# Reordering the head of a cosine-attention + MLP kernel: first pair's copies, third roots and a value load moved earlier

## The chip, the cores and the metric

One core of one Trainium2 chip. The metric is device time in microseconds (us); lower is better. Every run also lists the mean clock that TensorE was granted, as a share of full speed. All times below are in us unless marked otherwise.

## The reference, cut to what matters

```python
# q, k, v: (8 batches, 12 heads, 448 positions, 64) float32
q_n = q / (norm(q, axis=-1) + 1e-6);  k_n = k / (norm(k, axis=-1) + 1e-6)
attn = softmax(q_n @ k_n^T / 0.1)
x = (attn @ v) -> (3584 tokens, 768)
out = gelu_exact(x @ w_in) @ w_out          # 768 -> 2048 -> 768
```

## The kernel before

The kernel handles two heads at a time, a "pair"; six pairs make a batch. For each pair it squares queries and keys, sums the squares per row, takes roots, scales and rounds to bf16 (a 16-bit float), transposes (TensorE, then a copy by VectorE out of PSUM, the memory that TensorE writes to), multiplies scores, takes exponentials (ScalarE), and multiplies by the values. Then the batch goes through the MLP, whose first product is called `hp`. From the second batch on, all this preparation lies under dense matmuls of the MLP. Only in the first batch, about the first 38 us, is TensorE short of work. It is filled there with dummy matmuls, `spin`.

The code counts from 0, the texts count ordinals from the first: "third roots" and "third scaling" belong to index 2 (`roots(3)` brings the number done to three), and "squares of pair 3" are those of index 3, the only whole pair's squares on VectorE (of pair 0 it has the queries). "Sums" (`reduce`) are the sums of squares per row, on VectorE. A root is taken on ScalarE as half a logarithm and then an exponential, and VectorE makes its reciprocal, so "fourth logarithm" is the start of the fourth root. `upto(f, n)` calls `f` until `n` calls are done. In these traces each engine's instructions stand in the order in which they are written here.

```python
def square(g):
    ...
    elif g <= 2:
        nc.scalar.activation(sq, t, AF.Square)
    elif g == 3:
        nc.vector.tensor_tensor(sq, t, t, ALU.mult)     # two SBUF inputs
    else:
        nc.gpsimd.tensor_tensor(sq, t, t, ALU.mult)

def scale(g):          # two halves, queries and keys; all on GpSimd but half of pair 0
    ...
    for i, eng in enumerate((nc.vector if g == 0 else nc.gpsimd, nc.gpsimd)):
        eng.tensor_tensor(qkb[:, i]..., t[:, i], rn[:, i].to_broadcast(...), ALU.mult)

def spin(n):
    ...
    ps = mm_tile("spin")
    for _ in range(n):
        nc.tensor.matmul(ps[:CS, :S], lhsT=ident, rhs=blank, start=True, stop=True)

def attention_first():
    ...
    for g in range(HP):                       # HP = 6 pairs
        scores(g, 0)
        if g == 0:
            upto(square, 4)
            upto(reduce, 4)
            roots(3)
            upto(scale, 3)
            scores(g, 2, 1)
        if g < HP - 1:
            upto(transposes, g + 2)
        ...                                   # spin, value sums, scores(g, 2 or 3)
        upto(load_v, (2, 3, 3, 3, 3, 4)[g], NV)
        upto(load_wi, (1, 2, 3, 4, 4, 4)[g])
        ...
    ...                                       # the last values of the batch

# main program
...
upto(load_qk, 5)
spin(24)
...
upto(load_v, 1, NV)
upto(square, 1); upto(reduce, 1); roots(1); upto(square, 3); upto(scale, 1); upto(reduce, 2)
roots(2)
upto(scale, 2)
upto(load_v, 2, NV)
upto(load_wi, 1)
upto(transposes, 1)
spin(5)
upto(reduce, 3)
...                                           # attention_first, MLP, next batches
```

Values (`load_v`) and weights (`load_wi`) are loaded by GpSimd, each issue costing it about 0.8 us. `load_v` number 0 covers pair 0, number 1 pairs 1 and 2, number 2 pairs 3 to 5.

## Time and profile before

| | before |
|---|---|
| time, median of 3 (range) | 440.19 (439.91 to 441.44) |
| profiled run, granted clock | 439.89, 0.999 |
| first queries landed = VectorE's first squares start | 4.58 |
| first exponential starts | 12.75 |
| first MLP product `hp` starts | 38.52 |

The landing of the first queries varies between runs by up to 0.65 us whatever the kernel. So times of the head are compared below as distance from that landing: `hp` starts 33.95 after it here.

First, three stretches of 2 us of this kernel, from the view by stretches. The columns are the stretch and its length, busy time and instruction count of PE, PEld, DVE, ACT and POOL, then PEclk, the DMA share and GB/s:

```profile
14.00:16.00 2.00, 1.84 (x16) 0.97 (x14) 1.93 (x5) 1.97 (x5) 0.68 (x2) 1.00 1.12 235
16.00:18.00 2.00, 1.00 (x8) 0.51 (x9) 0.73 (x3) 1.97 (x5) 2.00 (x3) 1.00 1.13 236
18.00:20.00 2.00, 2.00 (x14) 1.09 (x15) 0.80 (x2) 1.08 (x2) 2.00 (x2) 1.00 1.25 236
```

Second, three rows of TensorE's timeline (start, length, engine, line, operation, tiles, shapes, count): two groups of fillers and the first `hp`.

```profile
14.87 0.96 PE L323 MATMUL spin<-blank,ident 112*112 112x448 bf16 x4
18.21 0.92 PE L323 MATMUL spin<-blank,ident 112*112 112x448 bf16 x4
38.52 0.74 PE L433 MATMUL hp<-x,wi 128*128 128x448 bf16 x3
```

The clock is full in all three stretches (1.00), and four fillers take 0.92 to 0.96.

### The profile page before, as it was taken

What the parts mean: (1) busy time and instruction counts of PE and PEld (TensorE: products, weight loads), DVE (VectorE), ACT (ScalarE), POOL (GpSimd) and SP (SyncE); (2) the same over time, 40 slices, a digit from 0 to 9 for tenths busy, and PEclk for the clock granted to TensorE, in tenths of its full rate; (3) what the DMA queues carried; (4) which work ended last, traced back from release to release, by engine and by line L of the source; (5) the groups of instructions that cost most, each with busy time, mean ns of one, the idle gap of its engine ahead of it and who ended that gap; (6) DMA issues with size and microseconds to landing.
All of it is one profiled execution on the core that took longest, in us unless ns stands there. A gap on an engine that the chain in (4) does not pass through costs nothing.

```text
span 438.1 us, 7927 instructions
## 1 busy us (share of the span) xinstructions
PE 426.8 (97%) x3294; PEld 215.7 (49%) x3294; DVE 164.8 (38%) x266; ACT 264.0 (60%) x380; POOL 203.3 (46%) x185
## 2 busy tenths in 40 slices
PE   7789999999999999999999999999999999999996
PEld 4344554445445554455544545445444554445563
DVE  4776313641355305552154501753055421341021
ACT  4796587646666467744767359655766457773300
POOL 2899834491834609291571906655190722300000
PEclk9999999999999999999999999999999999999999
DMA  9999999946683909766295843748077600911022
GB/s 201 237 241 209 180 178 211 265 105 135 109 160 88 226 4 114 171 119 149 29 159 134 159 109 53 172 121 208 1 130 153 134 2 1 132 43 31 1 72 72
DMA packets 83635, 54.97 MB, mean 125 GB/s; under 512 B 41872, under 2 KB 78608, under 8 KB 83600
## 3 DMA queue, kind: packets, MB, share of 16 engines
q1 hardware_dynamic: 66416, 42.35, 43.4%
q0 software_dynamic: 16784, 11.80, 19.1%
q8 instruction: 25, 0.41, 0.4%
q10 hardware_dynamic: 400, 0.33, 0.2%
q14 instruction: 10, 0.08, 0.1%
HBM read 45.61 MB, written 11.01 MB: 129 GB/s over the span
## 4 chain that ended last, share of the span: by engine, by line
PE 90%; DMA 5%; POOL 2%; DVE 1%; ACT 1%; SPq 0%; issue 0%; DVEq 0%
PE op L268 35%; PE hp L433 33%; PE st L206 11%; PE o L228 7%; PE sm L228 4%; DMA qk<-in_k_dram 3%; DMA v<-in_v_dram 2%; POOL qkb L176 1%; POOL sq L137 1%; SPq L107 0%; ACT pt L209 0%; DVE nq L149 0%; DVE x L246 0%; DVE rs L239 0%; DVE ot L279 0%
## 5 line engine op out<-in xcount | busy, mean ns | idle before, releaser
L209 ACT ACTIVATE pt<-st 112x896 bf16<-112x896 f32 x192 | 165.1, 913 | 50.0 <-PE st L206 49.6
L268 PE MATMUL op<-wo,g 128*128 128x384 bf16 x896 | 157.9, 327 | 0.0
L433 PE MATMUL hp<-x,wi 128*128 128x448 bf16 x768 | 147.0, 353 | 0.2 <-DVE x L246 0.2
L455 ACT ACTIVATE g<-hp 128x448 bf16<-128x448 f32 x128 | 66.9, 545 | 89.9 <-PE hp L433 89.6
L268 PEld LDWEIGHTS <-g 128*128 128x128 bf16 x896 | 81.9, 98 | 70.0 <-issue 21.0
L433 PEld LDWEIGHTS <-wi 128*128 128x128 bf16 x768 | 74.5, 98 | 72.1 <-issue 3.7
L176 POOL TENSOR_TENSOR qkb<-qk,rn 112x512 bf16<-112x512 f32 x95 | 96.8, 1045 | 11.8 <-DVE rn L167 11.7
L137 POOL TENSOR_TENSOR sq<-qk 112x1024 f32<-112x1024 f32 x44 | 82.3, 1888 | 5.8 <-DMA qk<-in_k_dram 5.6
L165 POOL TENSOR_SCALAR se<-sr 112x48 f32<-112x48 f32 x14 | 4.6, 326 | 150.2 <-ACT sr L164 150.2
L149 DVE TENSOR_REDUCE nq<-sq 112x16 f32<-112x1024 f32 x47 | 57.0, 1214 | 38.7 <-POOL sq L137 38.6
L206 PE MATMUL st<-qkT 64*112 64x448 bf16 x384 | 59.7, 374 | 2.6 <-ACT pt L209 1.9
L279 DVE COPY ot<-op 128x384 f32<-128x384 f32 x55 | 29.8, 543 | 79.2 <-PE op L268 79.2
L167 DVE RECIPROCAL rn<-se 112x48 f32<-112x48 f32 (+1 forms) x20 | 7.9, 393 | 99.7 <-POOL se L165 99.4
L228 PE MATMUL o<-pt,v 112*32 112x448 bf16 x768 | 41.8, 353 | 1.0 <-DMA v<-in_v_dram 1.0
L206 PEld LDWEIGHTS <-qkT 64*112 64x112 bf16 x384 | 21.5, 124 | 38.3 <-issue 34.5
L246 DVE TENSOR_TENSOR x<-o,rs 128x448 bf16<-128x448 f32 x48 | 27.8, 620 | 5.0 <-PE o L228 2.7
L228 PEld LDWEIGHTS <-v 112*32 112x32 bf16 x768 | 20.3, 97 | 17.1 <-DMA v<-in_v_dram 1.2
L235 DVE STREAM_TRANSPOSE tr<-sm 128x448 f32<-128x448 f32 x24 | 15.5, 646 | 34.8 <-PE sm L228 34.8
L228 PE MATMUL sm<-pt,ones 112*32 112x448 bf16 x384 | 23.1, 355 | 0.0
L323 PE MATMUL spin<-blank,ident 112*112 112x448 bf16 x46 | 13.3, 439 | 2.9 <-DVE qkT L194 1.5
L239 DVE STREAM_TRANSPOSE rs<-rc 128x448 f32<-128x448 f32 x24 | 15.5, 645 | 0.8
L120 POOL DMA_DIRECT2D v<-in_v_dram x17 | 14.0, 823 | 0.0
(37 smaller groups left out, 80.0 us busy)
## 6 DMA issues: line engine op xcount, KB each, us to landing
qk<-in_q_dram SPq DMA_DIRECT2D x48, 224.0 KB, 5.8
qk<-in_k_dram SPq DMA_DIRECT2D x47, 224.0 KB, 6.1
v<-in_v_dram POOLq DMA_DIRECT2D x15, 336.0 KB, 6.8
wi<-in_moe_w_in_dram POOLq DMA_DIRECT2D x4, 768.0 KB, 11.5
wo<-in_moe_w_out_dram POOLq DMA_DIRECT2D x4, 768.0 KB, 20.7
out_dram<-ot SPq DMA_DIRECT2D x7, 336.0 KB, 3.5
out_dram<-ot SPq DMA_DIRECT2D x8, 288.0 KB, 2.6
out_dram<-ot SPq DMA_DIRECT2D x8, 240.0 KB, 3.0
```

Of the source, the lines that this page charges most:

```text
L137: nc.gpsimd.tensor_tensor(sq, t, t, ALU.mult)
L149: nc.vector.tensor_reduce(nq, sq, mybir.AxisListType.X, ALU.add)
L176: eng.tensor_tensor(qkb[:, i].rearrange("p c h d -> p h c d"), t[:, i], rn[:, i].to_broadcast([CS, 2, NC, D]), ALU.mult)
L206: nc.tensor.matmul(st[:CS, h, :S], lhsT=qkT[rows, 1, c, :], rhs=qkT[rows, 0, :, :], start=True, stop=True)
L209: nc.scalar.activation(pt, st[:CS, :, :S], AF.Exp, scale=inv_tau)
L228: nc.tensor.matmul(bank_t[g, n][r:r + 32, :S], lhsT=w, rhs=pt_t[g + j, c][:, h, :], start=(c == 0), stop=(c == NC - 1), tile_position=(0, r))
L235: nc.vector.transpose(tr.rearrange("p b r -> p (b r)"), bank_t.pop((g, 0))[:, :S])
L246: nc.vector.tensor_tensor(x_t[b][:, p + n - 1, :], bank_t.pop((g, n))[:, :S], rs, ALU.mult)
L268: nc.tensor.matmul(ps[:, :NH], lhsT=g_t[sb][:, kf, t * 128:(t + 1) * 128], rhs=wo[:, kf, ni * NH:(ni + 1) * NH], start=(kf == 0), stop=(kf ...
L279: nc.vector.tensor_copy(ot[:, lo:hi], ps[:, :NH])
L433: nc.tensor.matmul(hps[m], lhsT=wi[:, kd, m * 128:(m + 1) * 128], rhs=x_t[b][:, kd, :], start=(kd == order[0]), stop=(kd == order[-1]))
L455: nc.scalar.activation(g_t[sb][:, m, hf * S:(hf + 1) * S], hps.pop(m), AF.Gelu)
```

## The change

Its intent: VectorE copies the first pair's transposes while it would else wait for the second pair's root, so scores and exponentials start earlier; the third roots come ahead of the fourth sums, so GpSimd starts the third scaling earlier; value and weight loads move to where GpSimd idles, and the late value load that TensorE waited for is issued about 11.5 us earlier (25.60 before, 14.04 after).

```diff
 attention_first, g == 0:
             upto(square, 4)
-            upto(reduce, 4)
             roots(3)
             upto(scale, 3)
+            upto(load_wi, 1)
             scores(g, 2, 1)
 ...
-        upto(load_v, (2, 3, 3, 3, 3, 4)[g], NV)
+        upto(load_v, (3, 3, 3, 3, 3, 4)[g], NV)
 main program:
     upto(reduce, 2)
+    upto(load_v, 2, NV)
+    upto(transposes, 1)
+    spin(2)
     roots(2)
     upto(scale, 2)
-    upto(load_v, 2, NV)
-    upto(load_wi, 1)
-    upto(transposes, 1)
-    spin(5)
+    upto(load_v, 3, NV)
     upto(reduce, 3)
```

The fourth sums are then written after the first transposes of the second pair (`upto(reduce, ...)` in the loop).

## The prediction

> **What bounds the kernel now.** I read the page's busy shares first, then TensorE's waits after the first batch, then the chain of waits of the first 60 us, then the timeline row by row.
>
> ```profile
> PE 426.8 (97%) x3294; PEld 215.7 (49%) x3294; DVE 164.8 (38%) x266; ACT 264.0 (60%) x380; POOL 203.3 (46%) x185
> PEclk9999999999999999999999999999999999999999
> ...
> core 0: us, PE busy (x) PEld busy (x) DVE busy (x) ACT busy (x) POOL busy (x), PEclk, DMA share, GB/s
> 38.50:438.00 399.50, 395.31 (x3012) 199.63 (x3008) 139.89 (x220) 237.35 (x340) 174.04 (x153) 1.00 0.59 116
> ...
> engine line waited for: us in total, times, longest us
> PE hp L433 <- DVE x L246: 0.2, 1, 0.2
> ```
>
> TensorE is busy 97% at the full granted clock. From 38.5 us, where the first MLP product `hp` starts, to the end, all its waits come to 0.2 us. The change touches only the instructions before that. So its worth is the number of microseconds by which `hp` starts earlier, if nothing later takes them back. At best it is some part of 38.5 us, of which most is work; 2% would be 8.8 us.
>
> The head is a chain that changes engines (start, length, what):
>
> ```profile
> 16.91 0.72 POOL qkb L176
> 17.91 1.88 POOL sq L137
> 19.80 2.00 POOL qkb L176 x2
> 21.80 1.85 POOL sq L137
> 23.65 1.95 POOL qkb L176 x2
> 25.60 7.08 DMA v<-in_v_dram
> 32.73 0.93 PE o L228 x14
> ```
>
> GpSimd works without a gap from 15.9 to 25.6 us, only then issues the value load, and TensorE waits for its landing. Ahead of that, the rows that the reordering concerns:
>
> ```profile
> 10.51 0.18 DVE L160 TENSOR_REDUCE se<-root 112x16 f32<-112x32 f32 x1 [0.97 <-ACT root L159]
> 11.28 1.11 PE L323 MATMUL spin<-blank,ident 112*112 112x448 bf16 x5 [1.54 <-DVE qkT L194]
> 12.56 1.63 DVE L135 TENSOR_TENSOR sq<-qk 112x1024 f32<-112x1024 f32 x1
> 15.91 2.04 POOL L176 TENSOR_TENSOR qkb<-qk,rn 112x512 bf16<-112x512 f32 x2 [1.32 <-DVE rn L167]
> 19.50 1.72 ACT L209 ACTIVATE pt<-st 112x896 bf16<-112x896 f32 x2 [0.92 <-PE st L206]
> 32.73 0.93 PE L228 MATMUL o<-pt,v 112*32 112x448 bf16 x14 [0.96 <-DMA v<-in_v_dram]
> 34.03 3.34 ACT L209 ACTIVATE pt<-st 112x896 bf16<-112x896 f32 x4 [1.08 <-PE st L206]
> ```
>
> VectorE idles 0.97 us for the second pair's root, although the first pair's transposes (done at 9.33 and 9.73) lie ready to be copied.
>
> **What the Trainium skill says.** (1) "Perfetto Trace Analysis", Optimization Strategy: a kernel can have several regimes, and one finds the gaps on the engine that matters in that regime and what releases them. This trace agrees: by the stretches view TensorE is busy 8.36, 6.73 and 16.40 us in 0 to 10, 10 to 20 and 20 to 38.5, so idle for 7.0 us, and almost never after. (13.3 us of that busy time are fillers, the `spin` row of the page.) (2) "SBUF — State Buffer", Who interferes with whom: a VectorE instruction with two SBUF inputs contends with a GpSimd one that reads SBUF; the first to issue holds the shared pair for its whole length. The trace agrees: the squares of pair 3 start on VectorE at 12.56, GpSimd's scaling ends at 13.10, and the squares end at 14.18, 1.08 after that, 1.63 in all. (3) "DMA: Bandwidth & Descriptors", Issuing engines are not separate DMA queues: all loads share 16 engines and interleave. The DMA share is 1.17 at 10 to 20 us and 1.15 at 20 to 38.5, so moving loads redistributes landings and adds no bandwidth. (4) "TensorE: Matmul & The Clock Gate", HAM clock gate: an idle window of about 3.4 us halves the clock. Only three filler matmuls go, and the wait that they border gets shorter; here a wait of 1.54 us left the next ones at 0.19 us spacing, so I give this nothing.
>
> **The change, part by part** (times in us; "b" is before).
>
> 1. First pair's copies first. They fall into the 0.97 wait: first at 9.44 (b 10.89), second at 9.77 to 10.15 (b ends 11.52). The second pair's root still comes at 10.51, so that costs nothing. Fillers go from five to two, 0.19 each: scores start at 10.30 (b 12.31), the first exponential at 10.74 (b 12.75): 2.0 earlier. The second pair's scaling on GpSimd stays at 11.06 to 13.10.
>
> 2. Third roots ahead of fourth sums. The squares of pair 3 now issue at 12.02, but behind the same GpSimd scaling, by point (2): they end at 14.18 as before. Next on VectorE come the third roots (14.10, b 15.35) rather than 1.2 of sums. Their logarithm sits on ScalarE behind two earlier exponentials, done at 12.91, so it is ready. Reciprocal ends 14.57 (b 15.82), third scaling on GpSimd starts 14.65 (b 15.91): 1.25 earlier. The fourth sums end 16.17 (b 15.44), so the fourth logarithm starts at about 16.23 against 16.41: here ScalarE keeps only 0.2 of its 2.0, and idles 1.4 for it.
>
> 3. ScalarE's later wait of 0.92 goes. It stood because the third pair's transposes waited for the scaling; those now end at 16.95, four fillers follow, scores at 17.80, and the exponential follows without a gap at 18.29 (b 19.50).
>
> 4. The weight load leaves the idle time before the third scaling and comes after it, into the solid GpSimd chain: 0.78. Scaling ends 16.69, load to 17.4, squares of pair 4 at 17.43 (b 17.91). So GpSimd's lead shrinks from 1.25 to 0.48. It is also what sets the fifth logarithm (20.63, b 21.11) and all TensorE work to about 31: lead 0.48.
>
> 5. The value load of pairs 3 to 5 goes from 25.60 to about 13.1, in the gap before the third scaling. Two effects. GpSimd is 0.83 shorter between the fifth and sixth scalings, which TensorE doesn't wait for (in before it was still at other matmuls when the sixth scaling ended, 29.25 against 29.42). And the value wait goes. In before the block of 16 matmuls starts at 31.41, stops after two of them until 32.73, and the next scores come at 33.59. With the lead of 0.48 it starts at 30.93 and takes 0.87, as 16 such matmuls do elsewhere in the chain: next scores at 31.80, a lead of 1.79.
>
> 6. Part of this is given back. The next scores wait for exponentials, now in a closed row: 32.36 to 35.69 on ScalarE (b 34.03 to 37.37). The scores that came at 35.81 come at 34.13. But the last value sums need the accumulator that VectorE's normalising frees: third value block 32.80 (b 34.11), normalised by 34.95 (b 36.26), last value block 35.02 (b 36.33). From there 2.19 of dense matmuls: `hp` at 37.21 against 38.52.
>
> Sum: 0.48 from the reordering (1.25 less 0.78 for the weight load), plus 1.31 of value wait, less 0.48 by ScalarE and the accumulator: 1.3.
>
> **Rivals.**
>
> (a) The lock goes the other way: the squares get the pair at 12.10, between two scalings. They end at 13.18, the second scaling's half slips to 14.2, the value load to 15.0, the third scaling starts at 15.05. GpSimd's lead is then 0.08 and the whole gain about 0.9: 439.3. For it: VectorE waits already when the first half ends. Against: the second half is dispatched 0.04 before the first ends.
>
> (b) Later landings don't move along. DMA is saturated to 64 us, its order changes but not its volume. The second output-weight load lands at 56.75 and is needed at 58.6, so at 57.3 after; the transposed tile of pair 9 lands at 70.95 and is first used at 71.53, so at 70.22. If that landing stays, 0.7 is lost and 0.6 is left: 439.6. For it: 6.9 us from issue to landing beside other loads. Against: its issue at 64.08 follows the scaling, which comes earlier too, and the weights ahead are issued earlier as well.
>
> (c) The early value loads push back loads that are needed. The pair-3 keys land at 10.86, before the early load of the second values, issued about 9.3 (a load issued at 6.14 landed only at 14.60), can get in; first input weights have slack: the second of them landed at 36.36, needed now at 37.21, and less lies ahead of it. If wrong, squares on GpSimd wait and the gain is nil: 440.2.
>
> (d) The value wait was the only one that counted, ScalarE closing up everywhere after: 2 or more, 438.2, if the accumulator's 0.4 is hidden too.
>
> **Range and chances.** Centre 1.2: 1.3 with a little off for (a) and (b), so 439.0 from 440.19. The three runs of before spread over 1.5, most within 0.3. Low 438.2 is rival (d), high 440.1 is (c) with its noise. 2% is out of reach either way: the head holds only 7.0 us of idleness and 13.3 of fillers, most of which cover the first loads; and to lose 8.8 the order would have to stall on a load.
>
> **What would show each step.** First exponential at 10.7; squares of pair 3 ending 14.2 (lock as before) or 13.2 (a); third scaling at 14.65; fourth logarithm hardly earlier, with 1.4 of ScalarE idle ahead of it; fifth logarithm 0.5 earlier; no wait on a value load in TensorE's list; a TensorE gap of about 0.4 before the last value block; `hp` at 37.2; after it still about 0.2 of waits. I am wrong if `hp` starts within 0.5 of 38.52, if TensorE's waits after it exceed 0.5, or if its matmuls are slower.

## The result, and the profile after

| | before | after |
|---|---|---|
| median of 4 runs, same rounds (range) | 440.78 (439.91 to 441.44) | 439.72 (439.53 to 440.31) |
| ratio of means, 95% interval | | 0.9979 (0.9955 to 1.0003) |
| granted clock of the runs | 0.999 in the profiled one | 0.991, 0.992, 0.996, 0.990 |
| first landing | 4.58 | 4.93 |
| first exponential, after the landing | 8.18 | 6.22 |
| `hp`, after the landing | 33.95 | 33.97 |

Ratios here and below are the mean time of one kernel's fast runs over that of the other's in the same rounds, so they are not quite the ratios of the medians quoted.

The time lies in the predicted range, but the profile tells another story than the prediction: the first exponential is 1.96 earlier, as predicted, the value wait is gone, and yet `hp`, counted from the landing, starts not a moment earlier. Something in the head ate all of it. The page of the changed kernel, its clock line and PE's busy share:

```profile
PE 428.9 (98%) x3291; PEld 216.1 (49%) x3291; DVE 164.6 (38%) x266; ACT 264.4 (60%) x380; POOL 204.3 (47%) x185
...
PEclk9699999999999999999999999999999999999999
```

PE is busy 2.1 us longer than before (428.9 against 426.8) with three instructions fewer. The second digit of the clock line, about 11 to 22 us, is 6: before it was 9. The view by stretches, the same columns as above:

```profile
14.00:16.00 2.00, 1.85 (x9) 0.99 (x10) 1.26 (x2) 0.82 (x2) 1.99 (x4) 0.52 1.19 243
16.00:18.00 2.00, 2.00 (x10) 0.67 (x9) 0.93 (x3) 1.23 (x4) 1.98 (x3) 0.50 1.24 258
18.00:20.00 2.00, 2.00 (x12) 1.15 (x9) 1.00 (x2) 1.24 (x2) 2.00 (x2) 0.50 1.22 241
20.00:22.00 2.00, 2.00 (x10) 0.83 (x9) 0.84 (x1) 1.21 (x2) 2.00 (x3) 0.77 1.32 248
```

A clock of 0.50 is half speed. The trace's clock record has it from 14.09 to 20.92, that is for 6.83 us (the 0.52 and 0.77 fit: 1.91 and 0.92 us of these two stretches at half speed). TensorE's timeline shows what that does:

```profile
14.15 0.55 PE L192 MATMUL tp<-ident,qkb 112*128 112x112 bf16 x4 [1.33 <-POOL qkb L176]
15.18 1.74 PE L323 MATMUL spin<-blank,ident 112*112 112x448 bf16 x4
18.50 1.70 PE L323 MATMUL spin<-blank,ident 112*112 112x448 bf16 x4
38.90 0.36 PE L433 MATMUL hp<-x,wi 128*128 128x448 bf16 x1
```

Four fillers take 1.74 and 1.70 where they took 0.96 and 0.92. And the chain of waits, which before ran through GpSimd to the value load, now runs through slow fillers:

```profile
4.93 0.70 DVE sq L131
...
11.07 3.03 POOL qkb L176 x2
14.10 0.05 issue
14.15 0.55 PE tp L192 x4
...
15.25 1.67 PE spin L323 x4
...
18.71 1.49 PE spin L323 x4
```

A filler was free while TensorE had nothing to do. At half clock it pushes real work back.

The chain shows a second surprise: the second scaling, two instructions, takes 3.03 in place of 2.04. GpSimd's and VectorE's timelines:

```profile
11.07 3.02 POOL L176 TENSOR_TENSOR qkb<-qk,rn 112x512 bf16<-112x512 f32 x2 [0.68 <-DVE rn L167]
14.87 2.05 POOL L176 TENSOR_TENSOR qkb<-qk,rn 112x512 bf16<-112x512 f32 x2
```

```profile
11.98 1.21 DVE L135 TENSOR_TENSOR sq<-qk 112x1024 f32<-112x1024 f32 x1
```

The squares of pair 3 ended at 13.19 after 1.21; before they took 1.63, because they had to wait for GpSimd. Now it is GpSimd that waits: its second half took 2.02 (12.07 to 14.09) against 1.04 for one elsewhere. That is rival (a).

After the head nothing is given back. TensorE's waits from 37 us to the end are

```profile
PE o L228 <- DVE x L246: 0.2, 1, 0.2
PE hp L433 <- DVE x L246: 0.2, 1, 0.2
```

and every later TensorE instruction stands 0.37 to 0.38 later than in the trace before, about the 0.35 by which the first landing was later. So the whole story lies before `hp`.

### The profile page after: what moved, and what is told of

The parts are those of the page before. It is cut to its first block, busy times and chain, and to the rows that moved or that the text cites. A ratio compares the mean times of both kernels' runs of the same rounds, so it can differ in the third digit from the quotient of the medians.

```text
span 438.5 us, 7921 instructions
## 1 busy us (share of the span) xinstructions
PE 428.9 (98%) x3291; PEld 216.1 (49%) x3291; DVE 164.6 (38%) x266; ACT 264.4 (60%) x380; POOL 204.3 (47%) x185
## 4 chain that ended last, share of the span: by engine, by line
PE 93%; DVE 2%; ACT 2%; POOL 1%; DMA 1%; issue 0%; DVEq 0%; POOLq 0%
PE op L268 35%; PE hp L433 33%; PE st L206 12%; PE o L228 8%; PE sm L228 4%; ACT pt L209 1%; POOL qkb L176 1%; DMA qk<-in_q_dram 1%; PE spin L323 1%; PE tp L192 1%; DVE x L246 0%; DVE nq L147 0%; DVE nq L149 0%; ACT lq L155 0%; POOL v L120 0%
## 5 line engine op out<-in xcount | busy, mean ns | idle before, releaser
L176 POOL TENSOR_TENSOR qkb<-qk,rn 112x512 bf16<-112x512 f32 x95 | 97.8, 1055 | 11.3 <-DVE rn L167 11.0
L206 PE MATMUL st<-qkT 64*112 64x448 bf16 x384 | 60.9, 380 | 1.9 <-ACT pt L209 1.7
```

The costliest lines, as they stand in the source:

```text
L176: eng.tensor_tensor(qkb[:, i].rearrange("p c h d -> p h c d"), t[:, i], rn[:, i].to_broadcast([CS, 2, NC, D]), ALU.mult)
L206: nc.tensor.matmul(st[:CS, h, :S], lhsT=qkT[rows, 1, c, :], rhs=qkT[rows, 0, :, :], start=True, stop=True)
```

## The experiments

The first theory after the result: the change gains about 0.9 to 1.1 in the head, as rival (a) says, and the half clock takes it away again; the clock falls because TensorE is busy too little for too long early in the head. Its rivals: the fall is chance and costs nothing; or the moves themselves are worth nothing, because ScalarE or the landing of loads sets the end. "hp" below is the start of `hp` after the first landing, from the run's profile; a list of clocks is over its runs. By the rule of 2% the verdict of every run in the table is "same"; what follows are smaller differences, read with their intervals and clocks.

| run (chip) | mean of fast runs | ratio (95%) | clocks | hp |
|---|---|---|---|---|
| e1_fill5 (12) | 439.59 | 0.9997 (0.9976 to 1.0018) | 0.994 to 0.998 | 34.36 |
| e2_before_fill2 (12) | 439.80 | 1.0002 (0.9982 to 1.0022) | 0.990 to 0.999 | 33.69 |
| e3_value_only (12) | 439.45 | 0.9996 (0.9967 to 1.0026) | 4 runs 0.999 or 1.0, 2 below | 33.02 |
| e4_order_only (12) | 439.70 | 1.0000 (0.9974 to 1.0026) | 0.996 to 0.999 | 33.51 |
| e0_after_again (11) | 439.83 | 0.9995 (0.9977 to 1.0012) | 0.990 to 0.992 | 34.03 |
| e5_gap_fill (11) | 438.70 | 0.9969 (0.9952 to 0.9986) | 0.999 or 1.0 | 32.88 |
| e6_squares_scalar (11) | 438.43 | 0.9961 (0.9939 to 0.9983) | 0.999 or 1.0 | 32.03 |
| e7_value_earlier (11) | 437.84 | 0.9949 (0.9930 to 0.9969) | 0.998 to 1.0, one slow run | 31.81 (slow run) |
| e8_best_again (3) | 437.61 | 0.9945 (0.9929 to 0.9960) | 0.998 to 1.0 | 31.61 |
| e9_copies_late (3) | 440.02 | 0.9999 (0.9972 to 1.0025) | 3 runs 0.999 or 1.0, 3 below | 34.35 |
| e10_weights_early (3) | 437.40 | 0.9940 (0.9925 to 0.9955) | 0.999 or 1.0 | 31.56 |
| e11_before_filled (3) | 439.19 | 0.9980 (0.9965 to 0.9996) | 0.999 or 1.0 | 33.22 |

The kernel before ran beside them, 11 times on each chip: means 439.71 (chip 12), 440.33 (11), 440.07 (3). Its own clock falls too: 18 of these 33 runs had a clock below 0.998. Their mean is 440.51, that of the other 15 is 439.47. So one fall costs it about 1 us, and "before" is a mix of two states. The mix differs by chip (3, 6 and 9 of 11 runs on chips 12, 11 and 3), so part of a ratio in the table is the clock of the kernel before. The changed kernel fell in all ten runs that it had.

**e1_fill5: the changed kernel with five fillers instead of two.**

```diff
     upto(transposes, 1)
-    spin(2)
+    spin(5)
```

> The changed kernel with five filler matmuls ahead of the first scores again, instead of two. Filler theory: with three fillers fewer TensorE did too little in a window of about 3.4 us before 14.1 us, the clock was halved for 6.8 us and that cost about 1 us; with five the granted clock is back at 0.999 in the runs, first scores about 0.57 later than in the changed kernel, the MLP start at 37.4 to 38.0, time about 0.7 to 1 us below the changed kernel's. Rival, lock theory: the pause comes from the wait of 1.33 us for the second pair's scaling, which GpSimd lost to VectorE's squares; then fillers ahead of it don't matter, the clock still falls to 0.99 and the time is that of the changed kernel or up to 0.5 us more.

The clock still fell, in five of six runs, and not at the same place: in the profile from 23.60 to 27.01. A miss for the idea that the three removed fillers were the cause. Two rows of TensorE's timeline:

```profile
13.97 0.37 PE L192 MATMUL tp<-ident,qkb 112*128 112x112 bf16 x4 [1.23 <-POOL qkb L176]
24.55 0.62 PE L323 MATMUL spin<-blank,ident 112*112 112x448 bf16 x1
```

The gap of 1.23 behind the slow second scaling is still there, and the fillers ahead of the scores delay the exponentials (6.78 after the landing in place of 6.22). The single filler at 24.55 takes 0.62, where one takes 0.35 at full clock.

**e2_before_fill2: the kernel before with two fillers instead of five.**

```diff
     upto(transposes, 1)
-    spin(5)
+    spin(2)
```

> The kernel before with two fillers instead of five at the same place, nothing else. Filler theory: its clock falls too, to 0.990 to 0.996, and it is about 0.5 to 1.5 us slower than before. Rival, lock theory: no squares ahead of the scaling, so the clock stays at 0.999, and the scores come up to 0.57 us earlier, of which at most 0.3 us reaches the end.

The clock fell in five of six runs (in the profile from 13.81 to 17.23), against 3 of 11 of the kernel before on that chip. That points to fillers at this place helping the clock, on few runs. But the mean, 439.80, is no worse than before's 439.71: scores came earlier too (first exponential 7.75 after the landing, before 8.18), and the value wait was 0.6 instead of 1.0. Mixed.

**e3_value_only: the kernel before, only the third value load moved.** It goes with the second, into GpSimd's idle time after the second scaling; the order of everything else stays.

```diff
     upto(scale, 2)
-    upto(load_v, 2, NV)
+    upto(load_v, 3, NV)
     upto(load_wi, 1)
```

> The kernel before with the third value load alone moved into GpSimd's idle time before the third scaling; VectorE's order, fillers and the weight load as before. My sum: the value wait of 1.3 us goes, 0.5 of it given back at the exponentials and the accumulator, so the MLP starts about 0.8 us earlier (37.7), clock 0.999, time 0.8 us below before. Rival, contention theory: the earlier load delays the first weight load or the keys, and less than 0.3 us is left.

GpSimd's timeline has the two loads side by side, and TensorE's has the block of sixteen value matmuls without the stop:

```profile
12.85 1.53 POOL L120 DMA_DIRECT2D v<-in_v_dram  x2
```

```profile
31.21 0.94 PE L228 MATMUL o<-pt,v 112*32 112x448 bf16 x16
```

`hp` starts 0.93 earlier than before. Over all runs the time shows nothing (0.9996), as two of the six had a fallen clock. The four at full clock took 438.48 to 438.94, mean 438.75; the eight full-clock runs of the kernel before on the same chip have a mean of 439.49. So this one line is worth about 0.7 us where the clock holds.

**e4_order_only: the changed kernel with five fillers and the third value load at its old place.**

```diff
-    spin(2)
+    spin(5)
     roots(2)
     upto(scale, 2)
-    upto(load_v, 3, NV)
 ...
-        upto(load_v, (3, 3, 3, 3, 3, 4)[g], NV)
+        upto(load_v, (2, 3, 3, 3, 3, 4)[g], NV)
```

> The changed kernel with five fillers, but the third value load at its old place behind the fifth scaling: the reordering on VectorE and the weight load's place alone. If the squares of pair 3 take the shared pair first, as in the changed kernel's profile (squares end 13.2, second scaling's half takes 2.0 us), GpSimd's lead is about 0.1 us and the time within 0.2 us of before; if my first reading had held (squares end 14.2), 0.5 us below before. The value wait of about 1 us is in TensorE's list again in either.

The value wait is back with 0.8, the second scaling again takes 3.02, the clock fell in four of six runs (half from 14.61 to 18.02 in the profile), and the ratio is 1.0000. Over all runs the reordering without the load shows no gain in time. But `hp` is 0.44 earlier than in the profile before, fallen clock and all, and its two runs at 0.998 and 0.999 took 438.59 and 438.99, mean 438.79, which is 0.7 below the full-clock runs of the kernel before: as much as e3. Two runs do not settle it, so what the reordering is worth alone at full clock stays open.

**e0_after_again and e5_gap_fill: the clock itself.** e0 is the changed kernel, unedited, so that e5 has it on the same chip. e5 adds fillers only where TensorE waits: three ahead of the third scores of pair 0, five ahead of the second pair's transposes (the gap behind the slow scaling), three ahead of the fourth pair's.

```diff
-    def spin(n):
-        ps = mm_tile("spin")
+    def spin(n, aside=None):
+        ps = mm_tile("spin", aside=aside)
 ...
             upto(load_wi, 1)
+            spin(3, 0)
             scores(g, 2, 1)
+        spin((5, 0, 3, 0, 0, 0)[g], 0)
         if g < HP - 1:
             upto(transposes, g + 2)
```

> The changed kernel itself, beside the next three on one chip. Clock below 0.998 in most of its runs, since a window of 3.41 us around 9 to 14 us holds only 0.2 to 0.35 of TensorE streaming whatever the window's phase; time within 0.5 us of before.

> The changed kernel with fillers put where TensorE really waits: three ahead of the third scores of pair 0, five ahead of pair 1's transposes, three ahead of pair 3's. Activity theory (a window with less than about 0.4 of streaming halves the clock for the next): clock at 0.998 or above in most runs, the matmuls after 14 us at their full pace, MLP start 33.0 to 33.2 after the first load's landing as in the kernel with the value load alone, time 0.7 to 1.0 us below the changed kernel's on this chip. Rival (the clock falls with the phase of the run or with the chip, not with activity): clocks and times as for the changed kernel, plus nothing.

e0 repeats the result: clock fallen in six of six runs, half from 13.10 to 19.92 in the profile, `hp` 34.03. e5 held the full clock in six of six. Its fillers at the place of the slow ones, on TensorE's timeline, and its second scaling, on GpSimd's:

```profile
14.61 0.96 PE L323 MATMUL spin<-blank,ident 112*112 112x448 bf16 x4
```

```profile
10.90 3.02 POOL L176 TENSOR_TENSOR qkb<-qk,rn 112x512 bf16<-112x512 f32 x2 [0.99 <-DVE rn L167]
```

The fillers are back at 0.96 while the scaling is as slow as in the changed kernel. So the two effects are told apart. `hp` is 1.15 earlier than in e0, and the mean time 1.13 lower (438.70 against 439.83): the fallen clock cost the changed kernel 1.1 us, all that it had gained. Both runs are on the same chip and the edit adds eleven matmuls, so it is not that less work was done.

**e6_squares_scalar: e5 with the squares of pair 3 on ScalarE**, written behind the third roots, so that no VectorE instruction with two SBUF inputs meets the second scaling.

```diff
-        elif g <= 2:
+        elif g <= 3:
             nc.scalar.activation(sq, t, AF.Square)
-        elif g == 3:
-            nc.vector.tensor_tensor(sq, t, t, ALU.mult)
 ...
-                upto(square, 4)
                 roots(3)
+                upto(square, 4)
```

> The same with the squares of pair 3 on ScalarE, behind the third roots: VectorE then has no instruction with two SBUF inputs beside GpSimd's second scaling. Lock theory: the second half of that scaling takes 1.04 us and not 2.02, the third scaling starts about 1 us earlier than in the changed kernel, the fourth logarithm about 0.8 earlier, and 0.3 to 0.8 us of it reaches the MLP start. Rival: ScalarE pays 1.0 us for the squares ahead of the exponentials, and it is the closed row that sets the end, so no gain or a loss of up to 0.3 us against the run before.

GpSimd's timeline:

```profile
11.23 2.04 POOL L176 TENSOR_TENSOR qkb<-qk,rn 112x512 bf16<-112x512 f32 x2 [1.11 <-DVE rn L167]
14.05 2.05 POOL L176 TENSOR_TENSOR qkb<-qk,rn 112x512 bf16<-112x512 f32 x2
```

The second scaling is back at 2.04, the third starts 9.38 after the landing instead of 10.25, and `hp` comes 0.85 earlier than in e5: the lost microsecond of the lock goes nearly whole into `hp`. The mean time fell by 0.27 only, and its six runs spread over 1.7, so on time alone this step is not settled.

**e7_value_earlier and e8_best_again: e6 with the third value load beside the second, in GpSimd's wait for the second roots** rather than between the second and third scaling. The two kernels are the same, on two chips.

```diff
     upto(reduce, 2)
-    upto(load_v, 2, NV)
+    upto(load_v, 3, NV)
     upto(transposes, 1)
```

> The run before with the third value load issued beside the second one, in GpSimd's wait for the second roots, and not between second and third scaling. GpSimd's third scaling then starts as soon as the third roots are there, 0.4 us earlier than in the run before; 0.2 to 0.4 us of it reaches the MLP start, 36.5 to 37.0 with a first load at 4.6. Rival: the load ahead of the later keys delays a square on GpSimd, no gain.

> The best kernel so far again (gap fillers, squares of pair 3 on ScalarE, value load in the earlier wait), for a profile in the fast state, and as the base of the next two. Clock 0.998 or above, MLP start 31.8 after the first load's landing, time about 437.8, 0.5 to 0.6% below before.

The third scaling starts 8.97 after the landing (e6: 9.38) and `hp` 31.61 (32.03). Ratios 0.9949 and 0.9945. e7's profiled run was slow (448.83, clock 0.949) and is set aside; it is the only such run, and the other five have a mean of 437.84. Its clock record shows 0.949 from 4.43 us to the end and no stretch at half speed before the end of the kernel, so this is not the fall studied here; what made it slow stays open.

**e9_copies_late: e8 with the copies put back behind the second roots.**

```diff
-    upto(transposes, 1)
-    spin(2)
     roots(2)
     upto(scale, 2)
+    upto(transposes, 1)
+    spin(2)
     upto(load_v, 3, NV)
```

> The same, but the first pair's copies on VectorE behind the second pair's roots, as in before. If the copies' order is worth what its place in the chain says, the first exponential comes about 1.3 us later; ScalarE has 0.5 to 1.5 us of waits further on that take it up, so 0.3 to 1.0 us at the MLP start. Rival: the value load and the lock were all there was to gain, and it is within 0.2.

The first exponential is back at 8.18 after the landing, as before the change. TensorE's timeline has the gap back:

```profile
11.25 0.84 PE L323 MATMUL spin<-blank,ident 112*112 112x448 bf16 x2 [1.60 <-DVE qkT L194]
```

Those two fillers take 0.84: the clock fell at 11.35 here. Three of six runs fell. The other three took 438.64 to 439.22, mean 438.92, against 437.61 for e8: at full clock the copies-first order is worth 1.3 in this kernel. Part of that may be that the squares, now on ScalarE, stand behind the exponentials that wait for the copies: they start 10.26 after the landing, against 8.29 in e8. In the kernel of the change, with the squares on VectorE, its share cannot be read from this.

**e10_weights_early: e8 with the first two value loads early and the first weight load in the wait for the second roots**, so that nothing stands between the third scaling and the squares of pair 4.

```diff
-    upto(load_v, 1, NV)
+    upto(load_v, 2, NV)
     upto(square, 1)
 ...
     upto(load_v, 3, NV)
+    upto(load_wi, 1)
     upto(transposes, 1)
```

> The best kernel with the first weight load out of GpSimd's solid chain: second values beside the first, weights beside the third values in the wait for the second roots. If the 0.78 that the load takes between third scaling and the squares of pair 4 sits on the path, the fifth logarithm comes 0.8 earlier and 0.2 to 0.6 reaches the MLP start. Rival: the load ahead of the keys of pairs 7 and 8 pushes them back, or ScalarE's closed row sets the end by now, and it is within 0.2.

GpSimd goes from the third scaling (13.25 to 15.25) straight to the squares of pair 4:

```profile
15.25 1.89 POOL L135 TENSOR_TENSOR sq<-qk 112x1024 f32<-112x1024 f32 x1
```

That is 10.97 after the landing; in e8 it was 11.78. Of those 0.8 us the fifth logarithm sees 0.24 (14.74 after the landing, 14.98 in e8), `hp` 0.05 and the mean time 0.2, the latter within the spread of the runs. So the place of the weight load was not on the path, at least not in this kernel. It is the fastest kernel: 437.34 median, 0.6% below the kernel before, with full clock in all runs. Against the two full-clock runs of the kernel before on that chip (mean 439.30) it is 0.4%; the rest is the clock.

**e11_before_filled: the kernel before, with fillers only.** Six in place of idleness after the first transposes (in another PSUM buffer, so that they don't wait for the copies), three ahead of the third scores, three ahead of the third pair's transposes.

```diff
     upto(transposes, 1)
+    spin(6, "st")
     spin(5)
 ...
             upto(scale, 3)
+            spin(3, 0)
             scores(g, 2, 1)
+        spin((0, 3, 0, 0, 0, 0)[g], 0)
```

> The kernel before with fillers in its own waits (six while the first copies are awaited, three ahead of the third scores, three ahead of pair 2's transposes), order and loads as before. Activity theory: its clock stays at 0.998 or above in all runs, and its mean falls by 0.3 to 0.8 us, to that of before's runs at full clock; the changed kernel with gap fillers is then about 1 us below it, which is the change's worth without the clock. Rival: no difference to before.

Full clock in five of five runs, 439.19 against 440.07 for the unedited kernel on the same chip: 0.9 faster without any useful instruction moved, near the 1.0 that its fallen runs lose. Its profile had `hp` at 33.22, 0.73 earlier than the profile before though both are at full clock; part of that is a value wait of 0.4 instead of 1.0, as that load landed earlier in this run. That the filled kernel of the change would be about 1 us below this one is not met: e5 has 438.70, 0.5 below, on another chip.

**What makes the clock fall.** The clock changes at multiples of 3.41 us, counted from an instant that differs from run to run. For each such window I worked out from the trace which share of it TensorE was streaming: 0.19 us for a matmul of 448 columns (the spacing of fillers at full clock), 0.05 for a transpose of 112, twice that at half clock, and the two heads' score matmuls, which run side by side, counted once. In the changed kernel the window 10.68 to 14.09 has three pairs of score matmuls and four transposes, 3 x 0.19 + 4 x 0.05, which is about 0.22 of 3.41.

```
windows ahead of a fall to half clock        share
  changed kernel   10.68 to 14.09             0.22
  e0               9.68 to 13.10              0.33
  e2               10.40 to 13.81             0.35
  e4               11.19 to 14.61             0.34
  e9               7.94 to 11.35              0.14
  e1               20.19 to 23.60             0.40
lowest window that stayed at full clock
  e1               9.95 to 13.36              0.39
  e3               9.30 to 12.71              0.44
  before           14.38 to 17.79             0.46
  e5               8.07 to 11.49              0.49
  e6, e8, e10, e11                            0.53 and above
```

Every share of 0.35 or less went with a fall, every share of 0.44 or more with none; between them e1 has one of each, and in the wrong order (0.39 stayed, 0.40 fell). Left out of the count, the transposes explain this: without them the six windows ahead of a fall have 0.03 to 0.29 and every window of the head that stayed has 0.33 (e3, 12.71 to 16.13) or more, e1's two being 0.29 and 0.34. No experiment tested transposes alone. The longest wait that reaches into one of the windows ahead of a fall is 1.7 us (e2), and 1.60 inside one (e9). The rule is read off a dozen profiles, after the fact; that the busy share is the cause and not only a companion is supported by e5 and e11, whose edits add fillers and nothing else. That the windows lie differently in each run explains why the kernel before falls in some runs and not in others; that is argued, since the other runs left no trace.

## Why the prediction was right or wrong

The time was right (439.0 predicted, range 438.2 to 440.1, measured 439.72 and again 439.97), and so was "within 2%". But the hit is luck. The mechanism was to start `hp` 1.3 earlier, and counted from the landing it started 0.02 later; the time fell, by 0.9 between the means of the first comparison and by 0.5 in the second, since part of the runs of the kernel before had a fallen clock themselves. The mechanism was right in part only, and the range was wide enough to take both errors.

**The step that failed: "Only three filler matmuls go, and the wait that they border gets shorter ... so I give this nothing."** The clock fell in ten of ten runs of the changed kernel and cost it 1.1 us (e5 against e0). I had looked for one idle window; the runs show that a thin window with no gap above 1.33 is enough. Putting the three fillers back does not mend it (e1). The gap behind the slowed scaling has to be filled as well (e5), and the prediction did not see that gap, since it had the lock the other way.

**Step 2, the lock, failed; rival (a) held.** I expected GpSimd's second half to hold the shared ports and the squares to end at 14.18, with the third scaling at 14.65 (10.07 after the landing). The squares got them in between, ended 13.19, and the third scaling started 9.94 after the landing in the changed kernel and 10.25 in e5; rival (a) has it at 15.05, or 10.47. That 9.94 is below my 10.07 is no point for my reading: the second scaling started earlier too (6.14 after the landing, before 6.48). From its start to the third scaling's are 3.80 in both runs, where I had 3.59 and rival (a) 3.99. The "against" of that rival, that the second half is dispatched 0.04 before the first ends, carried no weight: in all five profiles of this order the squares, which waited already, got the ports when the first half ended. At full clock rival (a)'s sum of 0.9 is close to what e5 shows: 1.07 of `hp`, and 0.82 of time (438.70 against 439.52, the mean of before's five full-clock runs on that chip).

**Steps that held.** Step 1: the first exponential came 1.96 earlier (2.0 predicted). Step 5: the value wait is gone, and alone it is worth 0.93 of `hp` (e3); the prediction's 1.31 less the 0.48 given back is 0.83. Step 6: the gap ahead of the last value sums is there, 0.2 instead of 0.4. The fourth logarithm came 0.25 earlier (0.2 predicted), but by another path: VectorE had its third reciprocal early and then waited 0.92 for transposes behind the slowed scaling, so this number is luck too.

**Steps that were mis-sized.** Reordering, 0.48 net: at full clock all of the change is worth 1.07 of `hp` (e5), the value load alone 0.93 (e3). The remaining 0.14 is what the reordering adds on top of the load while the lock is lost; it comes from single profiles, and the value wait alone differs by 0.6 between profiles of kernels without the early load (0.4 to 1.0), so it cannot be told from zero. By itself the reordering may be worth more (e4). With the squares off VectorE `hp` gains another 0.85 (e6). The fifth logarithm, predicted 0.48 earlier, is 0.29 earlier in e5 and 0.94 later in the changed kernel, where the half clock holds its sums and exponentials up. Step 4, the weight load at 0.78: it is in GpSimd's row with 0.80 as predicted, but e10 shows that taking it out brings `hp` 0.05.

**Step 3** (ScalarE's 0.92 wait goes) holds at full clock: in e5 ScalarE runs four exponentials in a row from 16.64. In the changed kernel it waits 1.56 for the slow scores instead.

**Rivals (b), (c), (d).** (b) and (c) are out: from `hp` on every TensorE instruction of the changed kernel is shifted by the same amount, no wait on a load appears, and the pair-3 keys had landed at 10.66, before their squares. (d), two or more, is out for this change.

The prediction named two of its own signs of error, `hp` within 0.5 of 38.52 (it was 38.90) and slower matmuls, and both appeared. What the range did not allow for is that the kernel before is itself a mix: about half of its runs carry the fallen clock. So the measured difference, 1.06 between the medians of the first comparison and a ratio of 0.9995 in the second, compares a kernel that always falls with one that falls half the time.

## What to carry to other kernels

Fillers that keep the clock up are part of the schedule: when a change shortens or moves a stretch, count again how much of every 3.4 us window TensorE streams, not only how long its longest wait is, and look at each run's granted clock before comparing times. Where a VectorE instruction with two SBUF inputs meets GpSimd's back-to-back instructions, don't bet on who gets the ports; move the instruction to a third engine, which here gave 0.85 us of `hp`. Test the parts of a reordering apart: here the value load alone gave 0.93 of the 1.07 us (e3), and a one-line experiment told it.

## What the Trainium skill lacked or had wrong

- "TensorE: Matmul & The Clock Gate", Part 1: The HAM clock gate, has the clock halved "after ≥1 idle window (~3.4µs)". The length of the window and that its phase differs from run to run agree with the runs (half clock lasted 3.41 or 6.83 us, the windows began at different times). But no window here was idle: the clock halved after windows with 0.14 to 0.40 of streaming and no gap longer than 1.7 us, and in the changed kernel none longer than 1.33. So the row leaves out how much streaming still counts as idle; in these kernels the limit lies near 0.4 of the window, or near 0.3 with transposes left out.
- The same page doesn't say how much streaming a window needs for the clock to come back. Here one window at half clock with a streaming share of 0.79 to 0.87 was enough in e1, e2, e4 and e9, while in the changed kernel a window with 0.83 was not and the next, with 0.91, was.
- "SBUF — State Buffer", Who interferes with whom: the exclusive lock agrees (GpSimd's half 2.02 instead of 1.04, or the squares 1.63 instead of 1.21). It lacks the case of two GpSimd instructions back to back: a VectorE instruction that was waiting when the first of them ended went in between, in all five profiles in which the squares started beside the first half (the changed kernel, e0, e1, e4, e5); where they started beside the second half (before, e2, e3, e11), GpSimd kept the ports to its end.
- No page says that a program on one core can have a slow run: one of the runs took 448.83 at a clock of 0.949, against 437.38 to 438.36 for the five others of the same kernel.
